# Spreading the read-back pairs among the computed ones, reordering the first chunk's loads, and loading the weights from another queue, in a fused attention and MLP kernel

## The chip, the cores and the metric

The kernel runs on one core of a Trainium2 chip. The metric is the device time of one execution in microseconds (us). Three runs of the kernel before took 1996.16, 1998.15 and 1998.2 us: the median is 1998.15 us.

## The reference

```python
# attention: u, v are (4, 3008, 256), z is (4, 3008, 64), float32
scores = (1.0 / S) * np.matmul(z, z.transpose(0, 2, 1))
attn = np.maximum(scores, 0.0) ** 2
x = (u * np.matmul(attn, v)).reshape(B * S, D)
# MLP on 12032 tokens: w_in is (256, 2048), w_out is (2048, 256)
h = x @ w_in
g = h * np.clip(h + 3.0, 0.0, 6.0) / 6.0
return (g @ w_out).astype(np.float32)
```

The scores are symmetric: the block of rows j and columns t is the transpose of the block of rows t and columns j. The two weights arrive as float64; the kernel reads them as pairs of 32-bit words.

## The kernel before, in words

**Tiles.** A batch has 3008 tokens, cut into 6 chunks of 512 columns (the last has 448); 4 batches make 24 chunks. For one chunk the 3008 rows are walked in 12 pairs of two 128-row tiles. The work of one pair in one chunk is a step: 24 x 12 = 288 steps, numbered g. Of every float32 operand a high part (fp32r) and the rest, a low part, are kept, and each product is made of three matmuls (low x high, high x low, high x high).

**A direct pair.** `scores` makes the block: 4 matmuls into a PSUM tile `s`, then ScalarE (ACT) applies the ReLU (`rt`) and the square in high form (`ah`), a square in full (`r2`, on ACT in the first three chunks, on VectorE, DVE, later), and DVE takes the rest (`al`). If the pair's rows belong to a later chunk (`keeps`), `keep` sends the full square to DRAM (`d<-r`, two transfers of 256 KB from SyncE's queue, SP), because its transpose is wanted there.

**A mirrored pair.** Where the pair's rows belong to an earlier chunk (`p // 2 < c`), nothing is computed: `fetch_pair` reads the kept block back (`l<-d`, four transfers of 128 KB on SP, two pairs ahead at most), `turn` transposes it on DVE (`rm`), ACT makes `ah` and DVE makes `al`. In chunk c the first 2c of 12 pairs are mirrored.

**The product with v.** `attend` adds the pair to the output `o`: 12 matmuls (two halves d, two tiles r, three products). The pairs of a chunk are taken in the order 0 to 11, so the mirrored ones all come first. After the last, DVE multiplies by u (`times_u`).

**The MLP.** From step `FIRST = 28` on, units of the MLP are put between the steps, some 1.4 a step: `up` (12 matmuls into `h`, then ReLU6 and the split) and `down` (12 matmuls into `y`).

**The order.** It is written out by hand in the loop at the end: in step g, `scores` for step g + `lead` (2 before step 28, then 1), `turn`, a number of weight operations, loads and splits for the next batch, `attend` of step g, units of the MLP. Engines run their instructions in that order.

**Weights.** They come in 16 pieces of 512 KB, two pieces ahead, each into one of the 5 buffers `r` that `rt`, `r2` and `rm` also use. A piece takes 8 DVE operations of `split64` and `finish64` (L101 to L133) and one copy on ACT (L117). `weight_work(n)` runs the next n of these: 1 before the first step, 2 a step in chunk 0, 4 a step up to step 27, then 5.

**The first chunk's loads.** z comes in 6 blocks, v in 12 pairs. In batch 0 v is loaded twice: as it is by SP, and rounded to the high part by GpSimd's queue (POOL), so that ACT needn't copy it; so are the z blocks 2 to 5. The loads of v, z, u and the weights stand in SP's queue between the `d<-r` and `l<-d`.

Of the kernel before, what the change touches and what calls it, by code (L numbers as in the profile page):

```python
# [13 lines left out]
B, S, D, DQK, DFF = 4, 3008, 256, 64, 2048  # L14
NT = B * S
P = 128
CH = 512
NCH = 6
# [12 lines left out]
def relu2_attention_then_hswish_mlp(  # L31
# [40 lines left out]
    def mm(out, lhsT, rhs, start, stop):  # L72
        nc.tensor.matmul(out, lhsT=lhsT, rhs=rhs, start=start, stop=stop)  # L73

    def split(hi, lo, raw, rounded=False):
        if not rounded:
            nc.scalar.copy(out=hi, in_=raw)  # L77
        nc.vector.tensor_tensor(out=lo, in0=raw, in1=f(hi), op=ALU.subtract)  # L78
# [69 lines left out]
    def fetch_w(kind, q):  # L148
        _, _, src, cols = w_piece(kind, q)
        if wide:  # L150
            raw = rpool.tile([P, 2, D, 2], U32, tag="r", name="wraw")
            nc.sync.dma_start(
                out=raw.rearrange("p k n w -> p k (n w)"),
                in_=src[:, :, 2 * cols.start:2 * cols.stop],
            )
        else:
            raw = rpool.tile([P, 2, D], F32, tag="r", name="wraw")
            nc.sync.dma_start(out=raw, in_=src[:, :, cols])
        raws["w", kind, q] = raw

    raws = {}
# [3 lines left out]
    def fetch_v(b, p):  # L165

        if b == 0 and p < NPAIR - 1:
            raw = vpool.tile([P, 2, D], F32, tag="vl", name="vraw")
        else:
            raw = stg.tile([P, 2, D], F32, tag="stg", name="vraw")  # L170
        vh = vpool.tile([P, 2, D], F32R, tag="vh", name="vh")
        vt[b, p] = vh
        raws["v", p] = raw
        j0 = p * 2 * P
        for dst, queue in ((raw, nc.sync), (vh, nc.gpsimd))[:1 if b else 2]:
            if p < NPAIR - 1:
                queue.dma_start(
                    out=dst, in_=v[b, j0:j0 + 2 * P, :].rearrange("(r q) d -> q r d", q=P)
                )
            else:  # L180
                queue.dma_start(out=dst[:, 0, :], in_=v[b, j0:j0 + P, :])
                for h in range(2):
                    queue.dma_start(out=dst[64 * h:64 * h + 64, 1, :], in_=v[b, j0 + P:S, :])

    def split_v(b, p):
        vh, raw = vt[b, p], raws.pop(("v", p))
        vl = vpool.tile([P, 2, D], F32R, tag="vl", name="vl")
        split(vh, vl, raw, rounded=b == 0)
        vt[b, p] = (vh, vl)

    def fetch_z(b, k):
        if b == 0:
            raw = xpool.tile([P, CH], F32, tag=("xh0", "xh1", "xl0", "xl1")[k % 4], name="zraw")
        else:
            raw = stg.tile([P, CH], F32, tag="stg", name="zraw")
        zx = zpool.tile([P, CH], F32R, tag="zx", name="zx")
        zy = zpool.tile([P, CH], F32R, tag="zy", name="zy")
        zt[b, k] = (zx, zy)
        raws["z", k] = raw
        cols = slice(k * CH, (k + 1) * CH)  # L200
        nc.sync.dma_start(out=raw, in_=zz[b, :, cols])
        if b == 0 and k > 1:
            nc.gpsimd.dma_start(out=zx[0:64], in_=zz[b, 0:64, cols])
            nc.gpsimd.dma_start(out=zy[64:128], in_=zz[b, 64:128, cols])
# [11 lines left out]
    def flush():  # L216
        urgent.clear()
        while late:
            late.pop(0)()

    kept, mirrored, turned, whole = {}, {}, {}, set()
    to_fetch = []

    def fetch_mirrored():

        while to_fetch and len(mirrored) < 2:
            b, c, p = to_fetch[0]
            if (b, p // 2, c) not in whole:
                return
            fetch_pair(*to_fetch.pop(0))  # L230
# [33 lines left out]
    def turn(b, c, p):  # L264

        if p // 2 >= c:
            return
        n = width(c)
        t = mirrored.pop((b, c, p))
        rn = rpool.tile([P, 2, CH], F32, tag="r", name="rm")[:, :, :n]  # L270
        nc.vector.transpose(  # L271
            out=rn.rearrange("p r (k e) -> p r k e", e=32),
            in_=t[:, :n // 32].rearrange("p k (r e) -> p r k e", r=2),
        )
        turned[b, c, p] = rn
        fetch_mirrored()

    def from_mirror(b, c, p):
        n = width(c)
# [79 lines left out]
    def av(b, c, p, d):  # L359

        n = width(c)
        if p == 0:
            bank = "y" if (b, c) == (0, 1) else "o"
            ot[d] = ps1.tile([P, CH], F32, tag=f"{bank}{d}", name=f"o{d}")
        o = ot[d][:, :n]
        ah, al = at[b, c, p]
        vh, vl = vt[b, p]
        dd = slice(d * P, d * P + P)
        for r in range(2):
            last = p == NPAIR - 1 and r == 1  # L370
            mm(o, vl[:, r, dd], ah[:, r, :n], p == 0 and r == 0, False)
            if not last:
                mm(o, vh[:, r, dd], al[:, r, :n], False, False)
            mm(o, vh[:, r, dd], ah[:, r, :n], False, last)
# [78 lines left out]
            nc.sync.dma_start(out=yt[e * P:(e + 1) * P, t0:t0 + n], in_=y[:, e, :n])  # L453

    chunks = [(b, c) for b in range(B) for c in range(NCH)]
    pairs = [(b, c, p) for b, c in chunks for p in range(NPAIR)]
    units = [("up", 0)]
    for q in range(NFP):
        units += [("up", q + 1)] if q + 1 < NFP else []
# [59 lines left out]
    def weight_work(n):  # L519
        for _ in range(n):  # L520
            next(w_ops, None)
# [39 lines left out]
    with tc.manual_schedule():  # L561
        nc.vector.memset(three, 3.0)
        fetch_z(0, 0)
        fetch_v(0, 0)
        split_z(0, 0)
        fetch_z(0, 1)
        fetch_v(0, 1)
        weight_work(1)
        split_v(0, 0)
        split_z(0, 1)  # L570
        scores(0, 0, 0)
        fetch_z(0, 2)
        fetch_v(0, 2)
        scores(0, 0, 1)
        fetch_v(0, 3)
        g_done = 2
        to_fetch += [(b, c, p) for b, c, p in pairs if p // 2 < c]
        g_turned = [2]
        for i, (b, c) in enumerate(chunks):
            ahead = b + 1 if c == NCH - 1 and b + 1 < B else None  # L580
            for p in range(NPAIR):
                g = i * NPAIR + p
                lead = 2 if g < FIRST else 1
                if i == 0:
                    if p + 1 < NPAIR:
                        split_v(0, p + 1)
                    if p % 2 == 0 and p // 2 + 2 < NCH:
                        split_z(0, p // 2 + 2)
                while g_done < min(g + lead + 1, len(pairs)):
                    scores(*pairs[g_done], square_on_act=i < 3)  # L590
                    g_done += 1
                if p > 3:
                    fetch_mirrored()
                if p < NPAIR - 1:
                    turn_next()
                if i == 0:
                    if p + 4 < NPAIR:
                        fetch_v(0, p + 4)
                    if p % 2 == 0 and p // 2 + 3 < NCH:
                        fetch_z(0, p // 2 + 3)  # L600
                    if p == 6:
                        load_u(*chunks[0])
                        load_u(*chunks[1])
                maybe_split()
                if g >= FIRST:
                    weight_work(5)
                elif p < NPAIR - 2:
                    weight_work(4 if i else 2)
                if ahead and p < NPAIR - 1:
                    if p:  # L610
                        split_v(ahead, p - 1)
                    if p < NPAIR - 2:
                        fetch_v(ahead, p)
                    if p % 2 == 1:
                        fetch_z(ahead, p // 2)
                    elif p:
                        split_z(ahead, p // 2 - 1)
                elif b and c == 0 and p < 4:
                    if p in (1, 2):
                        split_v(b, NPAIR - 3 + p)  # L620
                    if p < 2:
                        fetch_v(b, NPAIR - 2 + p)
                    if p == 2:
                        fetch_z(b, NCH - 1)
                    if p == 3:
                        split_z(b, NCH - 1)
                attend(b, c, p)
                turn_next()
                if p == NPAIR - 1:
                    avs[0] += 1  # L630
                total = len(pairs) - FIRST
                target = max(0, g + 1 - FIRST) * ((len(chunks) - 1) * NU - 4) // total
                mlp_units(target - units_done[0])
        mlp_units(1)
        maybe_split()
        mlp_units(len(chunks) * NU - units_done[0])
# [35 lines left out]
```

## Time and profile before

| | |
|---|---|
| median of 3 runs | 1998.15 us |
| the profiled execution: its own time | 1999.87 us |
| the profiled execution: span from first to last instruction | 1998.1 us |
| PE (TensorE) busy | 1960.8 us, 98% of the span |
| DVE, ACT busy | 1280.7 us (64%), 987.3 us (49%) |
| POOL busy | 14.2 us (26 instructions) |
| DMA | 178.14 MB, 89 GB/s over the span |
| mean granted TensorE clock | 0.992 |

PE is busy nearly throughout, so a change can only win where PE waits or runs below its full clock. Time is lost where the busy share of a stretch is below 1 or where PEclk is below 1.00.

### The profile page before, as it was taken

The numbers are of one execution on the slowest core, as the hardware profiler recorded it, in microseconds if no ns is written. First come the engines' busy times: TensorE is split into PE (matmuls) and PEld (weight loads), VectorE is DVE, ScalarE is ACT, GpSimd is POOL, SyncE is SP. The second block draws the span as 40 slices with busy tenths as digits, with TensorE's granted clock in tenths as the row PEclk, the third lists the DMA queues.
The fourth block names the chain that finished last, engine by engine and source line by source line (L and its number), as shares of the span: only waits on it lengthen the run. The fifth ranks groups of instructions, "written<-read, shape, count | busy, mean of one in ns | idle before, by whom it ended". The sixth has DMA issues, their size and how long they took to land.

```text
span 1998.1 us, 22059 instructions
## 1 busy us (share of the span) xinstructions
PE 1960.8 (98%) x8688; PEld 1637.4 (82%) x8688; DVE 1280.7 (64%) x1277; ACT 987.3 (49%) x1057; POOL 14.2 (1%) x26
## 2 busy tenths in 40 slices
PE   7899999999999999999999999999999999999999
PEld 5677788788888888888888888888888888888888
DVE  6798766676556566577565565657756565665654
ACT  6665444465444444456454454444555544444444
POOL 2000000000000000000000000000000000000000
PEclk8899999999999999999999999999999999999999
DMA  9754232424323233253332232324342223332300
GB/s 260 201 159 110 64 82 71 113 74 116 82 64 81 72 74 93 51 127 91 95 82 82 62 90 56 98 65 106 93 116 61 83 61 92 74 82 60 94 10 20
DMA packets 403271, 178.14 MB, mean 89 GB/s; under 512 B 250080, under 2 KB 385248, under 8 KB 403168
## 3 DMA queue, kind: packets, MB, share of 16 engines
q1 hardware_dynamic: 399232, 172.55, 34.3%
q0 software_dynamic: 3936, 4.20, 1.0%
q8 instruction: 68, 1.11, 0.2%
q14 instruction: 35, 0.29, 0.1%
HBM read 104.07 MB, written 72.61 MB: 88 GB/s over the span
## 4 chain that ended last, share of the span: by engine, by line
PE 89%; DVE 4%; DMA 3%; ACT 2%; issue 1%; SPq 1%; DVEq 0%; ACTq 0%
PE o L73 34%; PE h L73 24%; PE y L73 24%; PE s L73 7%; DMA zraw<-in_zz_dram 1%; DVE rm L271 1%; DMA vraw<-in_v_dram 1%; DVE al L287 1%; DVE rt L421 1%; ACT rt L420 0%; SPq L240 0%; ACT gh L77 0%; ACT rt L320 0%; DVE gl L78 0%; DMA d<-r 0%
## 5 line engine op out<-in xcount | busy, mean ns | idle before, releaser
L421 DVE SCALAR_TENSOR_TENSOR rt<-rt,h 128x1024 f32<-128x1024 f32 (+1 forms) x192 | 229.9, 1197 | 419.9 <-ACT rt L420 419.6
L420 ACT ACTIVATE rt<-h,three 128x1024 f32<-128x1024 f32 (+1 forms) x192 | 210.9, 1099 | 548.4 <-PE h L73 545.6
L73 PE MATMUL o<-ah,vl 128*128 128x512 f32 (+1 forms) x1152 | 448.5, 389 | 9.7 <-DVE vl L78 3.7
L73 PE MATMUL o<-ah,vh 128*128 128x512 f32 (+1 forms) x1152 | 447.6, 389 | 0.0
L73 PE MATMUL o<-al,vh 128*128 128x512 f32 (+1 forms) x1104 | 430.3, 390 | 7.8 <-DVE al L287 6.4
L73 PE MATMUL y<-gh,w_out_l 128*128 128x512 f32 (+1 forms) x768 | 296.2, 386 | 1.8 <-DVE w_out_l L133 1.7
L73 PE MATMUL y<-gl,w_out_h 128*128 128x512 f32 (+1 forms) x768 | 296.3, 386 | 1.0 <-DVE gl L78 1.0
L73 PE MATMUL h<-xh,w_in_l 128*128 128x512 f32 (+1 forms) x768 | 295.9, 385 | 0.0
L73 PE MATMUL y<-gh,w_out_h 128*128 128x512 f32 (+1 forms) x768 | 295.9, 385 | 0.0
L73 PE MATMUL h<-xl,w_in_h 128*128 128x512 f32 (+1 forms) x768 | 295.8, 385 | 0.0
L73 PE MATMUL h<-xh,w_in_h 128*128 128x512 f32 (+1 forms) x768 | 295.8, 385 | 0.0
L78 DVE TENSOR_TENSOR gl<-rt,gh 128x1024 fp32r<-128x1024 f32 (+1 forms) x192 | 230.6, 1201 | 80.5 <-ACT gh L77 77.9
L73 PEld LDWEIGHTS o<-ah,vl 128*128 128x128 f32 x1152 | 218.4, 190 | 57.6 <-ACT ah L285 5.8
L77 ACT CAST gh<-rt 128x1024 fp32r<-128x1024 f32 (+1 forms) x192 | 197.2, 1027 | 123.5 <-DVE rt L421 123.3
L73 PEld LDWEIGHTS o<-ah,vh 128*128 128x128 f32 x1152 | 218.6, 190 | 40.9
L73 PEld LDWEIGHTS o<-al,vh 128*128 128x128 f32 x1104 | 209.2, 190 | 51.5 <-DVE al L287 9.8
L320 ACT ACTIVATE rt<-s 128x1024 f32<-128x1024 f32 x168 | 171.2, 1019 | 131.9 <-PE s L73 126.9
L332 DVE TENSOR_TENSOR r<-rt 128x1024 f32<-128x1024 f32 (+1 forms) x140 | 169.9, 1214 | 95.8 <-ACT rt L320 95.8
L340 DVE TENSOR_TENSOR al<-r,ah 128x1024 fp32r<-128x1024 f32 x140 | 170.9, 1221 | 22.2 <-ACT r L330 8.7
L73 PEld LDWEIGHTS y<-gh,w_out_l 128*128 128x128 f32 x768 | 144.2, 188 | 29.9 <-DVE w_out_l L133 1.3
L73 PEld LDWEIGHTS y<-gl,w_out_h 128*128 128x128 f32 x768 | 144.2, 188 | 28.6 <-DVE gl L78 2.0
L287 DVE TENSOR_TENSOR al<-rm,ah 128x1024 fp32r<-128x1024 f32 (+1 forms) x120 | 141.1, 1176 | 40.0 <-ACT ah L285 39.9
(51 smaller groups left out, 1808.7 us busy)
## 6 DMA issues: line engine op xcount, KB each, us to landing
d<-r SPq DMA_DIRECT2D x220, 256.0 KB, 2.9
l<-d SPq DMA_DIRECT2D x320, 128.0 KB, 3.2
l<-d SPq DMA_DIRECT2D x160, 112.0 KB, 2.8
vraw<-in_v_dram SPq DMA_DIRECT2D x44, 256.0 KB, 3.4
u<-in_ut_dram SPq DMA_DIRECT2D x20, 512.0 KB, 4.3
out_dram<-y SPq DMA_DIRECT2D x40, 256.0 KB, 3.2
zraw<-in_zz_dram SPq DMA_DIRECT2D x24, 256.0 KB, 3.7
wraw<-in_w_in_dram SPq DMA_DIRECT2D x8, 512.0 KB, 4.5
```

The costliest lines, as they stand in the source:

```text
L73: nc.tensor.matmul(out, lhsT=lhsT, rhs=rhs, start=start, stop=stop)
L77: nc.scalar.copy(out=hi, in_=raw)
L78: nc.vector.tensor_tensor(out=lo, in0=raw, in1=f(hi), op=ALU.subtract)
L271: nc.vector.transpose(out=rn.rearrange("p r (k e) -> p r k e", e=32), in_=t[:, :n // 32].rearrange("p k (r e) -> p r k e", r=2),)
L287: nc.vector.tensor_tensor(out=al[:, :, :n], in0=rn, in1=f(ah[:, :, :n]), op=ALU.subtract)
L320: nc.scalar.activation(out=rn, in_=s[:, :, :n], func=AF.Relu, scale=1.0 / S)
L332: nc.vector.tensor_tensor(out=r2_of, in0=r_of, in1=r_of, op=ALU.mult)
L340: nc.vector.tensor_tensor(out=l_of, in0=r2_of, in1=h_of, op=ALU.subtract)
L420: nc.scalar.activation(out=rn, in_=h, func=AF.Relu, bias=three)
L421: nc.vector.scalar_tensor_tensor(out=rn, in0=rn, scalar=6.0, in1=h, op0=ALU.min, op1=ALU.mult)
```

## The change

1. `pairs_of(c)` gives the order of a chunk's pairs. In chunks 0 to 4 it begins with a direct pair and spreads the mirrored ones evenly among the direct ones; the last two places are direct. Chunk 1 goes 2, 3, 4, 5, 0, 6, 7, 8, 9, 1, 10, 11; chunk 2 goes 4, 5, 0, 6, 1, 7, 8, 2, 9, 3, 10, 11; chunk 5 and chunk 0 stay as they were. `av`, the list of pairs and `attend` follow that order.
2. In batch 0 v is loaded once, by SP; ACT makes the high part. The loads of z blocks 2 and 3 and of v pairs 2 and 3 come ahead of the first `scores`; those of z blocks 4 and 5 and of later v come at the start of a step, ahead of its `scores`. The loads of u come one step later.
3. The weights are loaded from POOL's queue. The first come in step 1. `weight_work` runs 2 operations in steps 1 to 9 of chunk 0; then, up to step 27, 5 in a step whose newest pair is direct and 1 where it is mirrored, none in a chunk's first step; from step 28 on 5, as before.

```diff
@@ fetch_w
-            nc.sync.dma_start(
+            nc.gpsimd.dma_start(
                 out=raw.rearrange("p k n w -> p k (n w)"),
                 in_=src[:, :, 2 * cols.start:2 * cols.stop],
             )
...
@@ fetch_v
-        for dst, queue in ((raw, nc.sync), (vh, nc.gpsimd))[:1 if b else 2]:
-            if p < NPAIR - 1:
-                queue.dma_start(
-                    out=dst, in_=v[b, j0:j0 + 2 * P, :].rearrange("(r q) d -> q r d", q=P)
-                )
...
+        if p < NPAIR - 1:
+            nc.sync.dma_start(
+                out=raw, in_=v[b, j0:j0 + 2 * P, :].rearrange("(r q) d -> q r d", q=P)
+            )
...
@@ split_v
-        split(vh, vl, raw, rounded=b == 0)
+        split(vh, vl, raw)
@@
+    def pairs_of(c):
+        if c == NCH - 1:
+            return list(range(NPAIR))
+        back, direct = list(range(2 * c)), list(range(2 * c, NPAIR))
+        order, gaps = direct[:1], len(direct) - 2
+        for k, p in enumerate(direct[1:]):
+            if k < gaps:
+                order += back[len(back) * k // gaps:len(back) * (k + 1) // gaps]
+            order.append(p)
+        return order
@@
-    pairs = [(b, c, p) for b, c in chunks for p in range(NPAIR)]
+    pairs = [(b, c, p) for b, c in chunks for p in pairs_of(c)]
@@ ahead of the loop
         fetch_z(0, 1)
         fetch_v(0, 1)
-        weight_work(1)
+        fetch_z(0, 2)
+        fetch_z(0, 3)
+        fetch_v(0, 2)
+        fetch_v(0, 3)
         split_v(0, 0)
         split_z(0, 1)
         scores(0, 0, 0)
-        fetch_z(0, 2)
-        fetch_v(0, 2)
         scores(0, 0, 1)
-        fetch_v(0, 3)
@@ in a step
                 if i == 0:
+                    if p + 4 < NPAIR:
+                        fetch_v(0, p + 4)
+                    if p < 2:
+                        fetch_z(0, p + 4)
...
-                if i == 0:
-                    if p + 4 < NPAIR:
-                        fetch_v(0, p + 4)
-                    if p % 2 == 0 and p // 2 + 3 < NCH:
-                        fetch_z(0, p // 2 + 3)
-                    if p == 6:
-                        load_u(*chunks[0])
-                        load_u(*chunks[1])
+                if i == 0 and p == 7:
+                    load_u(*chunks[0])
+                    load_u(*chunks[1])
                 maybe_split()
                 if g >= FIRST:
                     weight_work(5)
-                elif p < NPAIR - 2:
-                    weight_work(4 if i else 2)
+                elif 0 < p < NPAIR - 2:
+                    weight_work(2 if i == 0 else 1 if is_mirrored(*pairs[g_done - 1]) else 5)
...
-                attend(b, c, p)
+                attend(*pair)
```

**Where the instructions move.** The first place is SP's queue at the very start, batch 0, chunk 0 (`zraw`, `vraw` and `wraw` are loads of z, v and weights, `d01` the kept blocks of pairs 2 and 3). Before:

```order
L152 DMA wraw_118<-in_w_in_dram 128x2x512
L152 DMA wraw_120<-in_w_in_dram 128x2x512
L201 DMA zraw_141<-in_zz_dram 128x512
L177 DMA vraw_147<-in_v_dram 128x2x256
L177 DMA vraw_164<-in_v_dram 128x2x256
L257 DMA d01_184<-r2_181 512x1x128 x2
L177 DMA vraw_188<-in_v_dram 128x2x256
L201 DMA zraw_192<-in_zz_dram 128x512
```

With the change:

```order
L200 DMA zraw_116<-in_zz_dram 128x512
L200 DMA zraw_122<-in_zz_dram 128x512
L176 DMA vraw_128<-in_v_dram 128x2x256
L176 DMA vraw_131<-in_v_dram 128x2x256
L176 DMA vraw_167<-in_v_dram 128x2x256
L200 DMA zraw_170<-in_zz_dram 128x512
L270 DMA d01_193<-r2_190 512x1x128 x2
L176 DMA vraw_211<-in_v_dram 128x2x256
```

The weights are gone from this queue, and the fourth and fifth z block (`zraw_122`, `zraw_170`) stand ahead of the first kept block, where the fourth (`zraw_192`) stood behind it.

The second place is ACT in the same chunk, from pair 2 on. Before:

```order
L320 ACTIVATE rt_177<-s_172 128x1024
L329 ACTIVATE ah_178<-rt_177 128x1024
L330 ACTIVATE r2_181<-rt_177 128x8x4x32
L320 ACTIVATE rt_222<-s_217 128x1024
L329 ACTIVATE ah_223<-rt_222 128x1024
```

With the change:

```order
L336 ACTIVATE rt_186<-s_181 128x1024
L345 ACTIVATE ah_187<-rt_186 128x1024
L346 ACTIVATE r2_190<-rt_186 128x8x4x32
L77 CAST vh_129<-vraw_128 128x512
L336 ACTIVATE rt_228<-s_223 128x1024
```

Each step of chunk 0 has a fourth ACT instruction, the high part of v.

The third place is DVE where chunk 2 begins (`rm` and the `al` made of it are a mirrored pair's, the `al` of `r2` or `rt` a direct one's, `u` is `times_u`; `t0` and `wraw` are weight operations). Before:

```order
L271 STREAM_TRANSPOSE rm_972<-l_587 128x1024
L287 TENSOR_TENSOR al_992<-rm_972,ah_991 128x1024
L390 TENSOR_TENSOR u_449<-u_449,o0_649 128x512
L390 TENSOR_TENSOR u_449<-u_449,o1_656 128x512
L271 STREAM_TRANSPOSE rm_1007<-l_946 128x1024
L287 TENSOR_TENSOR al_1015<-rm_1007,ah_1014 128x1024
L271 STREAM_TRANSPOSE rm_1018<-l_974 128x1024
L131 TENSOR_TENSOR t0_846<-t0_846,w_out_h_93 128x512
```

With the change:

```order
L356 TENSOR_TENSOR al_958<-rt_956,ah_957 128x1024
L356 TENSOR_TENSOR al_982<-rt_980,ah_981 128x1024
L407 TENSOR_TENSOR u_480<-u_480,o0_642 128x512
L407 TENSOR_TENSOR u_480<-u_480,o1_649 128x512
L284 STREAM_TRANSPOSE rm_999<-l_673 128x1024
L303 TENSOR_TENSOR al_1007<-rm_999,ah_1006 128x1024
L356 TENSOR_TENSOR al_1031<-r2_1033,ah_1030 128x1024
L284 STREAM_TRANSPOSE rm_1040<-l_838 128x1024
```

The four mirrored pairs that opened the chunk one behind the other now have direct ones ahead of them and between them.

## Rows read from the trace of the kernel before

**Rows 1.** The page: the engines' busy time over the whole span, and the granted clock in 40 slices of 50 us each, in tenths.

```profile
PE 1960.8 (98%) x8688; PEld 1637.4 (82%) x8688; DVE 1280.7 (64%) x1277; ACT 987.3 (49%) x1057; POOL 14.2 (1%) x26
...
PEclk8899999999999999999999999999999999999999
```

**Rows 2.** Busy time of each engine by stretches of the span (us from its start): the stretch, its length, busy us and instructions of PE, PEld, DVE, ACT and POOL, then granted clock, DMA share and GB/s. The first stretch goes from the first matmul to the end of chunk 0's last product.

```profile
5.58:75.50 69.92, 55.98 (x191) 42.76 (x192) 45.11 (x60) 39.01 (x41) 9.67 (x16) 0.82 1.04 256
75.50:113.50 38.00, 38.00 (x166) 31.35 (x165) 34.16 (x50) 33.42 (x37) 0.00 (x0) 0.98 0.67 189
113.50:139.00 25.50, 22.50 (x87) 16.82 (x87) 22.34 (x30) 11.90 (x13) 0.00 (x0) 0.93 0.66 167
139.00:187.50 48.50, 48.50 (x216) 40.16 (x215) 40.47 (x55) 31.27 (x34) 0.00 (x0) 1.00 0.33 95
187.50:224.00 36.50, 31.95 (x135) 24.65 (x134) 32.87 (x41) 13.97 (x17) 0.00 (x0) 1.00 0.45 101
...
347.00:450.00 103.00, 99.11 (x449) 83.49 (x448) 73.87 (x80) 53.27 (x64) 0.00 (x0) 1.00 0.37 96
450.00:1950.00 1500.00, 1497.12 (x6698) 1256.39 (x6697) 936.23 (x877) 725.67 (x773) 0.00 (x0) 1.00 0.32 80
1950.00:1998.10 48.10, 44.67 (x217) 40.11 (x215) 20.03 (x20) 18.77 (x22) 0.00 (x0) 1.00 0.06 21
```

**Rows 3.** What PE waited for in the whole span: who waits, for whom, us in total, times, longest.

```profile
PE s L73 <- DVE zx L78: 7.4, 2, 5.6
PE o L73 <- DVE al L287: 6.4, 8, 1.8
PE s L73 <- issue: 6.2, 2, 3.9
PE o L73 <- DVE vl L78: 3.7, 2, 2.2
```

**Rows 4.** The chain of waits in the first 100 us: start, us, what.

```profile
1.65 6.68 DMA zraw<-in_zz_dram
...
18.76 11.65 DMA zraw<-in_zz_dram
...
50.99 3.90 issue
...
80.85 2.72 PE o L73 x12
83.57 0.91 PE s L73 x4
```

**Rows 5.** What ACT and DVE waited for in the first 76 us; two rows of ACT, then one of DVE.

```profile
ACT r L330 <- DMA d<-r: 6.2, 2, 3.9
...
ACT rt L320 <- DMA d<-r: 3.6, 1, 3.6
...
DVE zy L78 <- DMA zraw<-in_zz_dram: 11.5, 3, 6.4
```

**Rows 6.** DMA in the first 76 us: all packets, and issues with their number, KB each and median us from issue to landing.

```profile
DMA packets 26864, 18.91 MB, mean 249 GB/s; under 512 B 7917, under 2 KB 24045, under 8 KB 26861
...
d<-r SPq DMA_DIRECT2D x19, 256.0 KB, 5.1
...
vh<-in_v_dram POOLq DMA_DIRECT2D x11, 256.0 KB, 9.1
...
wraw<-in_w_in_dram SPq DMA_DIRECT2D x3, 512.0 KB, 11.0
```

**Rows 7.** The same from 80 to 112 us, in chunk 1.

```profile
d<-r SPq DMA_DIRECT2D x14, 256.0 KB, 2.9
wraw<-in_w_out_dram SPq DMA_DIRECT2D x3, 512.0 KB, 4.1
```

**Rows 8.** Groups of instructions from 76 to 112 us: line, engine, operation, out<-in, shapes, number, busy us, mean ns of one, idle time before.

```profile
L329 ACT ACTIVATE ah<-rt 128x1024 fp32r<-128x1024 f32 x10 | 10.6, 1063 | 0.3
L320 ACT ACTIVATE rt<-s 128x1024 f32<-128x1024 f32 x10 | 10.3, 1025 | 4.2 <-PE s L73 3.2 <-DMA d<-r 0.9
...
L340 DVE TENSOR_TENSOR al<-r,ah 128x1024 fp32r<-128x1024 f32 x7 | 8.5, 1219 | 0.0
...
L330 ACT ACTIVATE r<-rt 128x1024 f32<-128x1024 f32 x7 | 7.3, 1043 | 0.0
...
L106 DVE SCALAR_TENSOR_TENSOR t<-wraw,t 128x512 uint32<-128x512 uint32 x4 | 2.8, 693 | 0.1
...
L101 DVE TENSOR_SCALAR t<-wraw 128x512 uint32<-128x512 uint32 x5 | 2.1, 419 | 0.0
```

**Rows 9.** Instructions on the tile `vh` in the whole span: number, ns shortest/median/longest, first and last start. The first row is ACT's copy in batches 1 to 3, the second POOL's issue of the loads in batch 0.

```profile
L77 ACT CAST vh<-vraw x36: 598/618/622, 375.8 to 1465.2; 128x512 fp32r<-128x512 f32 x36
L177 POOL DMA_DIRECT2D vh<-in_v_dram x11: 726/730/844, 1.2 to 23.3; - x11
```

**Rows 10.** Instructions in order of time where chunk 2 begins: start, us, engine, line, operation, and in brackets the engine's idle time before and what ended it.

```profile
119.88 1.24 DVE L271 STREAM_TRANSPOSE rm<-l 128x1024 f32<-128x1024 f32 x1
121.21 1.05 ACT L285 CAST ah<-rm 128x1024 fp32r<-128x1024 f32 x1 [2.92 <-DVE rm L271]
122.29 1.23 DVE L287 TENSOR_TENSOR al<-rm,ah 128x1024 fp32r<-128x1024 f32 x1 [1.17 <-ACT ah L285]
123.43 1.28 DVE L390 TENSOR_TENSOR u<-u,o 128x512 f32<-128x512 f32 x2
```

More of the change, by code (lines that the diff above doesn't have):

```diff
@@ L157, in fetch_w @@
             raw = rpool.tile([P, 2, D], F32, tag="r", name="wraw")
-            nc.sync.dma_start(out=raw, in_=src[:, :, cols])
+            nc.gpsimd.dma_start(out=raw, in_=src[:, :, cols])
         raws["w", kind, q] = raw
@@ L174, in fetch_v @@
         j0 = p * 2 * P
-        for dst, queue in ((raw, nc.sync), (vh, nc.gpsimd))[:1 if b else 2]:
-            if p < NPAIR - 1:
-                queue.dma_start(
-                    out=dst, in_=v[b, j0:j0 + 2 * P, :].rearrange("(r q) d -> q r d", q=P)
-                )
[L180 to L183, printed above, removed]
+        if p < NPAIR - 1:
+            nc.sync.dma_start(
+                out=raw, in_=v[b, j0:j0 + 2 * P, :].rearrange("(r q) d -> q r d", q=P)
+            )
+        else:
+            nc.sync.dma_start(out=raw[:, 0, :], in_=v[b, j0:j0 + P, :])
+            for h in range(2):
+                nc.sync.dma_start(out=raw[64 * h:64 * h + 64, 1, :], in_=v[b, j0 + P:S, :])
     def split_v(b, p):
@@ L276, in turn, with is_mirrored @@
         fetch_mirrored()
+    def is_mirrored(b, c, p):
+        return p // 2 < c
     def from_mirror(b, c, p):
@@ L361, in av @@
         n = width(c)
-        if p == 0:
+        first = p == pairs_of(c)[0]
+        if first:
             bank = "y" if (b, c) == (0, 1) else "o"
@@ L370, in av @@
             last = p == NPAIR - 1 and r == 1
-            mm(o, vl[:, r, dd], ah[:, r, :n], p == 0 and r == 0, False)
+            mm(o, vl[:, r, dd], ah[:, r, :n], first and r == 0, False)
             if not last:
@@ L582, in relu2_attention_then_hswish_mlp @@
                 g = i * NPAIR + p
+                pair = pairs[g]
                 lead = 2 if g < FIRST else 1
                 if i == 0:
+                    if p + 4 < NPAIR:
+                        fetch_v(0, p + 4)
+                    if p < 2:
+                        fetch_z(0, p + 4)
                     if p + 1 < NPAIR:
```

## The prediction

> **What bounds the kernel now.** I read the page first: PE is busy for 98% of the span, and its clock is below full only in the first slices [rows 1]. Then the span by stretches, to see where the other 2% lie [rows 2]. At full clock a product takes 2.72 us and the four matmuls of a direct pair's scores 0.91 us, so a direct step needs 3.63 us of PE, a mirrored one 2.72 us, and one matmul 0.227 us [rows 4]. Chunk 0 holds 12 of each less two matmuls, 43.1 us, and takes 69.9 us: 26.8 us are lost, 13.9 in which PE is idle and 12.9 because the granted clock has a mean of 0.82, that is, stretches at 1.2 GHz among those at 2.4 [rows 2]. From 113.5 to 139 us 87 matmuls (19.7 us) take 25.5: 5.8 us lost. From 187.5 to 224 us 135 (30.6 us) take 36.5: 5.9 us lost. Between these nothing, and from 450 to 1950 us 2.9 us in all [rows 2]. So there are 38.5 us to win in the first 224 us, and next to nothing behind; the 3.9 us of the first chunk 5 and the 3.4 us of the tail lie where the order of pairs stays.
>
> What loses them: PE's waits name z's blocks (7.4 us), kept waiting by two loads that stand 6.7 and 11.7 us in the chain, and a piece of 3.9 us that the chain calls issue [rows 3, 4]. Behind these DVE waits 11.5 us for z, and ACT 9.8 us for a buffer `r` whose block is still on its way to DRAM [rows 5]. A block lands 5.1 us after issue there, against 2.9 us in chunk 1, because 18.91 MB move in 76 us, at 249 GB/s [rows 6, 7].
>
> **The change, part by part.**
>
> *Loads of chunk 0.* The second loading of v goes: 12 times 256 KB, 3.1 of 18.9 MB. The z blocks 3 and 4 stand ahead of the first kept block in SP's queue, so their 11.5 us of waiting should go [rows 5]. What is late next is ACT. It gets 12 copies of v at 0.62 us [rows 9], 7.4 us, and a step costs it 1.03 + 1.06 + 1.04 + 0.62 = 3.75 us [rows 8, 9], 0.12 us over PE's 3.63. Ten such steps and two weight copies (as long as v's) make 2.4 us, and the cold start with the first wait for an `al` I put at 2 us more, an estimate from the same rows (ACT's `ah` and DVE's `al` must follow before PE can go on, 2.3 us): 4.5 us lost is the lower end. The upper end is the DMA: 15.8 MB at the same 249 GB/s are 63.5 us, which end near 65 us instead of 75.5, so 16.3 us stay lost. The waits for `r` can't all go: eight `l<-d` still stand in SP's queue ahead of the kept block of pair 7, as before. I take 9.5 us, nearer to the lower end, since the waits on z and half of those on `r` vanish, and with them most of the idle time that brings the clock down to 1.2 GHz. **Gain 17.3 us**, ends 10.5 and 22.3. The copies on ACT I cost at nothing beyond that: ACT has 39.0 us of work in this stretch [rows 2], 46.4 with them, under some 53 us. Were that cover gone, it would be the whole 7.4 us.
>
> *Spread pairs and weights up to step 27.* Four mirrored pairs in a row cost PE its 5.8 us: `rm` 1.24, `ah` 1.05 and `al` 1.23 us follow each other, DVE idle 1.17 us for `ah`, so such a pair takes 3.5 us or more of a step in which PE has 2.72 us of work [rows 10]. Chunk 2 now begins with two direct pairs, and of the next four only two are mirrored. Against that, a direct step of chunk 1 gets five weight operations where it had four. An operation is 0.59 us (of eight, three at 0.42 and five at 0.69 [rows 8]), so DVE has 1.22 + 2.95 = 4.17 us in a step of 3.63 [rows 4, 8]. Seven such steps and two mirrored at 3.05 us exceed PE by 4.4 us; the three steps with no operations give 2.4 us back each. I leave 3 us lost. **Gain 2.8 us**, ends minus 1 and 5.8.
>
> *From step 28 to the last weight.* Up to step 27 the weights now get 18 + 37 + 11 = 66 operations, where they had 21 + 40 + 16 = 77. The 11 that are put off, 6.5 us, fall on a DVE that is idle 8.0 us from 139 to 187.5 us but only 3.6 us of the next 36.5 [rows 2]. For it speaks that the six mirrored pairs which open chunk 3 no longer stand together there. I leave 4.5 of the 5.9 us lost. **Gain 1.4 us**, ends minus 6.5 and 5.9.
>
> *The weights' queue.* SP loses 16 issues, POOL gets them, at 0.73 us each as for v [rows 9]; POOL does nothing else, so 11.7 us of issue lie beside everything. SP no longer stops for a free `r` ahead of a kept block; that gain is inside the terms above. What waits behind POOL's wait is the next weight alone, but behind DVE's wait for a weight stand all `al`.
>
> *The other batches.* A step there has 2.72 to 3.63 us of attention and over 3 us of MLP, which covers a mirrored pair's 3.5 us; nothing to win [rows 2], and 1.5 us either way.
>
> **Sum:** 17.3 + 2.8 + 1.4 = 21.5 us. Against the profiled execution, 1999.87 us with its span of 1998.1, that is 1978.4; that execution stands 1.7 us above the median of the runs, so against the median 1998.15 it is 1976.6 us. The ends together give 1962.6 and 1996.6, but they won't all fall on one side.
>
> **Rivals.**
>
> *The DMA stays the bound of chunk 0.* For it: the mean of 249 GB/s over 76 us [rows 6], and that pairs still write 512 KB a step in a shorter time, so `d<-r` may go on landing after 5 us, ACT go on waiting, and each idle stretch cost the clock again. Against it: 2.9 us in chunk 1 with the same writes [rows 7]. Then only 10.5 us come, and the rest nothing: 1987.6 us.
>
> *DVE gives part of it back.* PE reaches step 28 some 20 us earlier, with 11 operations more to do. If all 6.5 us show, 17.3 + 2.8 - 6.5 = 13.6 us remain: 1984.6 us. For it: DVE is 90% busy where 5.9 us are lost now [rows 2].
>
> *Slower: weights that come late through POOL.* A piece is fetched two ahead, that is, eight operations before it is needed, at five a step 1.6 steps or 5.8 us. Loads by POOL of half that size took 9.1 us to land in the first 76 us [rows 6]. If the full pieces do so throughout, each holds DVE for 3.3 us, with all `al` behind it; 12 pieces are loaded from step 12 on: 39.6 us, less the 17.3 us of chunk 0, 22.3 us slower: 2020.4 us. It turns from 1.4 us late a piece, at a landing of 7.2 us. Against it: those loads ran beside SP's at up to three ahead while weights by SP took 11.0 us, and later 4.1 us for a full piece [rows 6, 7].
>
> The Trainium skill (SBUF — State Buffer, section SBUF: two separate sides) speaks against the change in just this way: a VectorE instruction in a two-port mode locks GpSimd out of SBUF, so that GpSimd can't write the descriptors of its DMAs, and it tells to issue from SP or ACT instead. By that rule the loads would be late and the time be that of this rival. The trace doesn't bear it out so far: POOL's issues last 726 to 844 ns [rows 9], though DVE was busy for 45.1 of 69.9 us there [rows 2].
>
> *The change moves nothing*, because waits only take other names: 1998 us.
>
> **How the numbers follow.** The forecast gets 0.59, the DMA-bound chunk 0.16, DVE's giving back 0.13, late weights 0.08, nothing 0.04. The predicted time is the forecast's, 1976.6 us. The range 1966 to 1991 holds nearly all of the forecast and most of the next two. A measurement tells 0.2%, 4 us, from no change: faster by over that is 0.59 + 0.16 + 0.13, less 0.01 for the worst of the DMA's case, 0.87; within it 0.04; slower 0.09.
>
> **What would show it.** Right: chunk 0's last product ends near 60 us; DVE's waits on z gone, ACT's on `d<-r` below 5 us; the clock at 2.4 GHz for most of chunk 0; ACT over 85% busy there; no stop at the start of chunk 2; POOL with 24 loads. Wrong: the clock still falling three times in the first 60 us; DVE waiting for `wraw`; new waits of PE on `w_out_l` or `gl` before 210 us; more than 3 us lost in any 1000 us behind 450 us.

## The result and the profile after

The change makes the kernel slower: 2012.96 us median of 6 runs (2011.91 to 2014.09) against 1998.1 us for the kernel before, a ratio of 1.0076 [1.0065, 1.0086]. Forecast were 1976.6 us and faster. The profiled execution took 2013.18 us with a span of 2011.4, 13.3 us more than that of before.

The page answers to [rows 1]: the first two slices are nearly at full clock now, and the fifth, from 201 to 251 us, is not.

```profile
PE 1961.0 (97%) x8688; PEld 1637.5 (81%) x8688; DVE 1280.2 (64%) x1276; ACT 993.5 (49%) x1070; POOL 16.1 (1%) x28
...
PEclk9999899999999999999999999999999999999999
```

The stretches answer to [rows 2] (stretch, length, busy us and instructions of PE, PEld, DVE, ACT, POOL; granted clock, DMA share, GB/s). They are cut where chunk 0 ends and behind steps 27, 36 and 39.

```profile
3.00:63.60 60.60, 52.15 (x199) 40.80 (x200) 42.37 (x57) 48.76 (x57) 5.50 (x9) 0.94 0.93 245
63.60:131.10 67.50, 58.68 (x239) 45.71 (x238) 50.46 (x69) 43.14 (x48) 3.61 (x5) 0.95 0.55 145
131.10:192.20 61.10, 59.63 (x260) 48.25 (x259) 53.76 (x72) 34.35 (x37) 5.07 (x7) 1.00 0.46 121
192.20:234.20 42.00, 24.36 (x90) 18.84 (x89) 28.42 (x37) 12.80 (x15) 0.00 (x0) 0.80 0.22 49
234.20:454.00 219.80, 217.03 (x964) 181.64 (x963) 142.36 (x139) 106.07 (x118) 0.00 (x0) 0.99 0.35 87
454.00:1952.00 1498.00, 1493.64 (x6682) 1253.20 (x6681) 936.96 (x878) 723.18 (x771) 0.00 (x0) 1.00 0.33 80
```

Chunk 0's last product ends at 63.6 us instead of 75.5. From 63.6 to 131.1 PE idles 8.8 us, and from 192.2 to 234.2 it idles 17.6 of 42 us, at a mean clock of 0.80. What PE waited for, over the whole span, answers to [rows 3]:

```profile
PE y L73 <- DVE w_out_l L133: 9.9, 1, 9.9
...
PE h L73 <- DVE w_in_l L133: 7.7, 1, 7.7
...
PE s L73 <- DVE zx L78: 6.2, 1, 6.2
```

The 6.2 us are the first load of z. The two rows ahead of it are waits for the last DVE operation on a weight piece (L133), once for `h`, once for `y`. Before, PE waited 1.7 us in all for `w_out_l` and never for `w_in_l`. The two are the 17.6 us.

The chain of the first 70 us, against [rows 4], no longer names z's later blocks. It goes over ACT and four kept blocks on their way to DRAM, the first and the last of them here:

```profile
16.91 6.63 DMA d<-r
...
54.65 6.81 DMA d<-r
```

To see where time came and went I read when the product of each step ends, in both traces, and take the differences. By the end of chunk 0, and up to step 39, the new order has made the scores of two more pairs, since direct ones now open the next chunk; these 1.8 us (two times 0.91) are taken off, so the numbers compare equal work. Negative is gained (us); the term of the prediction stands beside.

| stretch | predicted | the change |
|---|---|---|
| to the end of chunk 0 | -17.3 | -13.7 |
| steps 12 to 27 | -2.8 | +7.3 |
| steps 28 to 39 | -1.4 | +19.0 |
| steps 40 to 287 | 0 | +0.3 |

### The profile page after: what moved, and what is told of

Its sections match the earlier page's. It is cut to its first block, busy times and chain, and to the rows that moved or that the text cites. A ratio compares the mean times of both kernels' runs of the same rounds, so it can differ in the third digit from the quotient of the medians.

```text
span 2011.4 us, 22062 instructions
## 1 busy us (share of the span) xinstructions
PE 1961.0 (97%) x8688; PEld 1637.5 (81%) x8688; DVE 1280.2 (64%) x1276; ACT 993.5 (49%) x1070; POOL 16.1 (1%) x28
## 4 chain that ended last, share of the span: by engine, by line
PE 87%; DVE 5%; ACT 4%; DMA 3%; issue 1%; SPq 0%; DVEq 0%; ACTq 0%
PE o L73 32%; PE h L73 24%; PE y L73 24%; PE s L73 6%; DMA d<-r 1%; ACT rt L336 1%; DMA zraw<-in_zz_dram 1%; ACT r L346 1%; ACT ah L345 1%; ACT rt L437 1%; DVE rt L438 1%; DVE gl L78 1%; DVE al L356 0%; DMA vraw<-in_v_dram 0%; DVE rm L284 0%
## 5 line engine op out<-in xcount | busy, mean ns | idle before, releaser
L73 PE MATMUL o<-ah,vl 128*128 128x512 f32 (+1 forms) x1152 | 447.2, 388 | 11.4 <-DVE vl L78 5.0
L356 DVE TENSOR_TENSOR al<-r,ah 128x1024 fp32r<-128x1024 f32 (+1 forms) x139 | 169.8, 1221 | 39.7 <-ACT r L346 26.2
L73 PEld LDWEIGHTS h<-xh,w_in_l 128*128 128x128 f32 x768 | 144.7, 188 | 35.9 <-issue 8.1
```

Of the source, the lines that this page charges most:

```text
L356: nc.vector.tensor_tensor(out=l_of, in0=r2_of, in1=h_of, op=ALU.subtract)
```

## The experiments

The question was which of three things costs the 26 us that the two middle rows lose: the numbers of weight operations in each step (66 called for by step 28, instead of 77), the new order of pairs, or POOL's queue. Results, with the gains by stretch as above (on equal work; medians and ratios are of all runs; the kernel before ran again beside the experiments, with medians of 1995.9 to 1997.1 us). The stretches are read from one profiled execution of each kernel. The runs of one kernel lie 1.2 to 6.4 us apart, so a difference of 2 or 3 us between two rows is not shown by the rows alone.

| kernel | median us | ratio to before | chunk 0 | 12 to 27 | 28 to 39 |
|---|---|---|---|---|---|
| the change | 2012.96 | 1.0076 | -13.7 | +7.3 | +19.0 |
| e1_counts | 1987.65 | 0.9956 [0.9941, 0.9971] | -13.3 | +0.2 | -0.6 |
| e9_counts_sp | 1986.37 | 0.9951 [0.9937, 0.9966] | -11.7 | -1.7 | -0.7 |
| e4_order | 1995.11 | 0.9991 [0.9981, 1.0] | -11.4 | +4.2 | +0.1 |
| e5_loads | 1989.76 | 0.9969 [0.9959, 0.9978] | -8.5 | -1.7 | +0.1 |
| e3_copy | 2013.35 | 1.0084 [1.0069, 1.0099] | -12.1 | +6.5 | +19.2 |
| e6_own | 2005.92 | 1.0053 [1.0038, 1.0068] | -17.0 | +2.7 | +19.3 |
| e2_six | 2006.5 | 1.0053 [1.0038, 1.0068] | -11.8 | +7.0 | +14.1 |
| e10_head | 2006.56 | 1.0053 [1.0038, 1.0068] | -12.7 | +8.2 | +11.4 |
| e11_two | 1993.78 | 0.9984 [0.9974, 0.9994] | -9.3 | +2.3 | -0.3 |
| e14_one_less | 1998.74 | 1.0007 [0.9998, 1.0017] | -11.1 | +2.4 | +7.8 |
| e12_own_counts | 1983.05 | 0.9931 [0.9916, 0.9946] | -17.7 | -0.6 | -0.6 |
| e13_own_counts_sp | 1985.66 | 0.9945 [0.993, 0.996] | -12.0 | -2.5 | -0.6 |

### The counts, the queue and the order

**e1_counts**: the change with the old numbers of weight operations, 77 by step 28 again.

```diff
-                elif 0 < p < NPAIR - 2:
-                    weight_work(2 if i == 0 else 1 if is_mirrored(*pairs[g_done - 1]) else 5)
+                elif i == 0 and 0 < p < NPAIR - 2:
+                    weight_work(3 if p < 4 else 2)
+                elif i and p < NPAIR - 2:
+                    weight_work(4)
```

> The change with the numbers of weight operations of before: 2 a step in chunk 0 (3 in steps 1 to 3, so that the total is the same), 4 a step in chunks 1 and 2 up to step 27, 77 in all by then instead of 66. Theory A (the numbers of operations cost the time: the last pieces come late at steps 38 and 39, 19.4 us there, and five a step lay ACT's copy of a weight behind DVE in steps 14 to 24, some 9 us): 2013 - 19 - 9 = 1985 us (1982 to 1990), PE's waits for w_in_l and w_out_l under 1 us. Rival B (weights come late because POOL loads them): the waits for w_in_l and w_out_l stay, over 2008 us. Rival C (mixed mirrored and direct pairs cost it): steps 12 to 27 still lose over 8 us, 1993 us or more.

Measured: 1987.65 us, 25.3 less than the change. The losses of both middle rows are gone. The stretches of steps 12 to 27 and 37 to 39:

```profile
64.00:124.60 60.60, 56.10 (x240) 44.08 (x238) 52.39 (x74) 43.20 (x47) 4.93 (x7) 1.00 0.68 167
...
185.60:208.00 22.40, 20.69 (x88) 15.99 (x86) 20.17 (x24) 12.11 (x14) 0.00 (x0) 1.00 0.23 48
```

The last takes 22.4 us for the work that takes 42.0 in the change. So the counts alone turn a gain into a loss.

**e9_counts_sp**: e1_counts with the weights loaded by SP (one word: `nc.sync` for `nc.gpsimd` in `fetch_w`).

> e1_counts (the change with the old numbers of weight operations, 1987.65 us) with the weights loaded by SP again. If POOL's queue is worth something in this order: 3 us or more slower than e1_counts. If not: within 2 us. If loads by POOL cost time (rival B): 3 us or more faster.

Measured: 1986.37 us, intervals that overlap. So POOL's queue is not what costs the change its 25 us. In e1_counts, a line of POOL:

```profile
L152 POOL DMA_DIRECT2D wraw<-in_w_in_dram x8 | 5.8, 727 | 65.8 <-DVE gl L78 13.2 <-DVE zx L78 10.7 <-DVE al L356 10.2
```

and the weight loads of the whole span (number, KB, median us from issue to landing):

```profile
wraw<-in_w_in_dram POOLq DMA_DIRECT2D x8, 512.0 KB, 5.6
wraw<-in_w_out_dram POOLq DMA_DIRECT2D x8, 512.0 KB, 5.4
```

and in e9_counts_sp:

```profile
wraw<-in_w_in_dram SPq DMA_DIRECT2D x8, 512.0 KB, 4.7
wraw<-in_w_out_dram SPq DMA_DIRECT2D x8, 512.0 KB, 4.5
```

Through POOL a piece lands 0.9 us later in the median, at 5.6 and 5.4 us, under the 7.2 us from which the rival would have begun.

**e4_order** and **e5_loads**: e4_order is e1_counts with the pairs in the old order 0 to 11 (`if c >= 0` for `if c == NCH - 1` in `pairs_of`); e5_loads has the weights on SP as well, so that only the loads of chunk 0 and the later first weights are new.

> The change with the numbers of weight operations of before and with the pairs in their old order 0 to 11; loads of chunk 0 and weights from POOL's queue as in the change. Against e1_counts it shows what the order alone does. If spreading is worth what the prediction took it for (the four mirrored pairs that open chunk 2 and the six of chunk 3): 3 to 8 us slower than e1_counts, some 1990 us. Rival C (spreading costs time): 3 us or more faster than e1_counts. If the order makes no difference: within 2 us of it.

> The kernel before with the new loads alone: v once with its high part from ACT, the new places of the loads of z, v and u, weights from SP's queue from step 1 on, the old order of pairs and the old numbers of weight operations (2 a step in chunk 0, 3 in steps 1 to 3, then 4). Against e4_order (1995.1 us), which has POOL's queue besides. If the queue is worth nothing: within 2 us of e4_order. If SP's stops for a free buffer were worth something: 3 us or more slower, 1998 us or more. If loads by POOL cost time (rival B): 3 us or more faster.

Measured: 1995.11 and 1989.76 us. The new loads alone, with SP, bring 0.3%. The order is no culprit: it brings 7.5 us with POOL (e4_order to e1_counts), 3.4 with SP (e5_loads to e9_counts_sp). But it doesn't bring it where it was forecast: with SP, steps 12 to 27 gain the same 1.7 us in either order, and the difference shows by the end of chunk 0, where chunk 1 opens. With the old order POOL is 5.4 us worse than SP, with intervals that do not overlap: the outcome that was named above for loads by POOL that cost time. Steps 12 to 27 lose 4.2 us where they gain 1.7. There, from 95 to 125 us, ACT in e4_order has a wait that e5_loads has not:

```profile
ACT rt L336 <- DMA d<-r: 3.2, 1, 3.2
```

and a kept block lands later, 3.8 us after issue, in e5_loads 2.6:

```profile
d<-r SPq DMA_DIRECT2D x5, 256.0 KB, 3.8
```

That SP, while it waits for a free `r`, keeps the weights from running beside the kept blocks is a reading; no run tests it. What the traces do show is where the queue counts. Chunk 1 (steps 12 to 23) takes 45.8 and 45.0 us with POOL (e4_order, e1_counts) and 41.3 and 43.0 with SP (e5_loads, e9_counts_sp); with buffers of their own for the weights, as in the last two runs below, it takes 43.0 with either queue. In chunk 0 POOL is ahead, by 1.6 to 5.7 us in the table. So the queue isn't neutral: two effects nearly cancel in the new order and don't in the old, and the loss hangs on the shared `r`. By what path is not shown.

### Steps 12 to 27

**e3_copy**: the change with ACT's copy (L117) of the newer piece kept back, so that it isn't run when an older piece is finished (`while len(copies) > pending` for `while copies` in `finish64`). ACT had waited 8.9 us for L114 at that copy, with `rt` behind it.

> The change with ACT's copy of a weight kept back: finish64 of one piece no longer issues the copy of the next piece, which then follows the next pair's squares, as it does before the change. Theory A2 (with five operations a step the copy is laid ahead of the next pair's rt on ACT while it waits for DVE's fourth operation behind this pair's al, so ACT and DVE take turns): ACT's waits of L117 for DVE t, 8.9 us in three from 75 to 125 us, fall below 2 us, steps 14 to 24 win 6 to 9 us, 2004 to 2007 us. Rival D (DVE has too much to do there, 4.17 us a step against PE's 3.63): the waits take another name, 2011 us or more. Rival B or A1 alone: 2013 us.

Measured: 2013.35 us, the same as the change. Of the copy's waits one of 1.2 us is left, and others have their time, ACT's and PE's from 64 to 130 us:

```profile
ACT rt L337 <- DMA d<-r: 5.1, 2, 3.2
ACT rt L337 <- PE o L73: 4.6, 1, 4.6
...
PE o L73 <- DVE al L357: 4.3, 5, 1.9
```

That theory fell. What stands behind `rt` in the change is a buffer: in order of time, before chunk 2,

```profile
110.23 0.62 ACT L117 CAST w_out_h<-t 128x512 fp32r<-128x512 f32 x1 [3.32 <-DVE t L114]
...
110.70 0.69 DVE L123 SCALAR_TENSOR_TENSOR w_out_l<-wraw 128x512 fp32r<-128x512 uint32 x1
...
111.47 1.02 ACT L336 ACTIVATE rt<-s 128x1024 f32<-128x1024 f32 x1 [0.62 <-DVE w_out_l L123]
...
113.64 0.50 PE L73 MATMUL o<-ah,vl 128*128 128x512 f32 x1 [2.06 <-ACT ah L345]
...
115.99 0.79 PE L73 MATMUL o<-al,vh 128*128 128x512 f32 x1 [1.85 <-DVE al L356]
```

L123 is the last operation that reads a raw piece; with it the piece's `r` comes free, and `rt` starts 0.08 us later. PE waits twice, and the granted clock is 0.5 (1.2 GHz) from 114.3 to 121.2 us.

**e6_own**: the change with two buffers of their own for the raw pieces, three left for `r`.

```diff
-    rpool = ctx.enter_context(tc.tile_pool(name="rpool", bufs=5))
+    rpool = ctx.enter_context(tc.tile_pool(name="rpool", bufs=3))
+    wrpool = ctx.enter_context(tc.tile_pool(name="wrpool", bufs=2))
...
-            raw = rpool.tile([P, 2, D, 2], U32, tag="r", name="wraw")
+            raw = wrpool.tile([P, 2, D, 2], U32, tag="wr", name="wraw")
```

> The change with two buffers of their own for the raw weights, the other uses of r keeping three of the five. Theory E (ACT's rt waits until DVE's operation L123 lets go of a weight's buffer, behind this pair's al and up to four other operations, so the pair that opens chunk 2 is 4 us late and the clock falls): that wait is gone, the end of step 24 comes 5 to 8 us sooner than in the change, step 28 too; what three buffers cost in the MLP is not the question, some 2007 us if nothing. Theory D (DVE is simply full in chunk 1 with five operations a step): the end of step 28 within 2 us of the change's 134.5 us, 2011 us or more.

Measured: 2005.92 us. Step 24, the first of chunk 2, ends at 112.9 us instead of 121.0; steps 12 to 27 lose 2.7 us instead of 7.3, and chunk 0 gains 3.3 us more. Steps 28 to 39 lose as before, so that is another cause.

### Steps 28 to 39

**e2_six**: the change with 6 operations a step from step 28 instead of 5 (`weight_work(6)`).

> The change with 6 weight operations a step from step 28 on instead of 5, nothing else. Theory A1 (the last pieces are split a step too late, because 11 operations fewer are done by step 28): the waits of PE for w_in_l and w_out_l, 17.6 us with a fall of the clock, go; 1996 us (1992 to 2000), and steps 12 to 27 stay as slow as they are. Rival B (loads by POOL come late): DVE can't go faster than the loads, 2010 us or more, with DVE waiting for wraw. Rival D (DVE is simply full from step 28 on): as much is lost spread over steps 28 to 38, over 2005 us.

**e10_head**: the change with 3 operations a step in chunk 0 instead of 2 (`3 if i == 0`), 75 by step 28.

> The change with 3 weight operations a step in chunk 0 instead of 2, so that 75 are done by step 28 instead of 66; five and one from chunk 1 on as in the change. Theory A1 (the stop at steps 38 and 39 comes only from being 11 operations behind when DVE is full): PE's waits for w_in_l and w_out_l, 17.6 us and a fall of the clock, go, steps 12 to 27 still lose 6 us or more, 1993 to 1998 us. If the five a step from step 28 on are too few whatever was done before: over 2005 us. If chunk 0 has no room on DVE: it ends 3 us or more later.

Measured: 2006.5 and 2006.56 us. In both the wait for `w_in_l` is gone, and the one for `w_out_l` stays, e2_six first:

```profile
PE y L73 <- DVE w_out_l L133: 9.3, 1, 9.3
```

```profile
PE y L73 <- DVE w_out_l L133: 7.1, 1, 7.1
```

Both waits were expected to go if being eleven operations behind were all; both times are over the 2005 us named for a DVE that is simply full. But the loss isn't spread over the steps, as it would be then: it sits in one wait. Ten operations (of the eleven) and nine are put back, and 9.3 and 7.1 of its 9.9 us stay, which doesn't look like DVE's amount of work. Counting in the program gives another cause. The unit `down` in step 38 needs w_out's seventh piece, whose last operation is the 127th called for. Before and in e1_counts 77 + 10 x 5 = 127 are called for by the end of step 37. The change has 66 + 50, e2_six 66 + 60 = 126, e10_head 75 + 50 = 125: there the last one is called for in step 38, and DVE takes it behind a unit's `rt` and `gl`, an `al`, a transpose and the split of x. The next two runs move one and two operations, some 35 steps earlier.

**e14_one_less**: e1_counts with one operation fewer (`3 if p < 3`), 126 by step 37.

> The changed kernel with the old counts of weight operations, but one operation fewer, in step 3 of chunk 0 (2 where the old counts have 3), so that all later ones stand one place later. Theory C: the last operation on w_out's seventh piece slips from the end of step 37 into step 38, behind an al, a transpose and the splits; PE waits 4 to 8 us for w_out_l about 205 us from the start, with part of it again in the clock: 1993 to 1998 us, where the old counts took 1987.65. Theory L: one operation of 0.6 us is put off, under cover: 1987 to 1989 us.

**e11_two**: e10_head with two more, in steps 1 and 2 (`(4 if p < 3 else 3) if i == 0`), 127 by step 37.

> The changed kernel with 4 weight operations in steps 1 and 2 of chunk 0 and 3 in steps 3 to 9, two more than in the run with 3 a step: 77 of them are called for by step 28, as before the change, but five and one a step stay in steps 12 to 27. Theory C (a threshold: the last operation on w_out's seventh piece has to be called for by step 37, or it stands behind the next pair's al and the splits of x, PE stops for it and its clock falls): the wait of y for w_out_l goes, step 39 ends 0 to 2 us after the kernel before instead of 8.7, and the whole takes 1997 to 2001 us. Theory L (only the amount of work on DVE counts): two operations are 1.2 us, so 2005 us and the wait stays at 5 us or more.

Measured: one operation less costs 11.1 us (1998.74 against 1987.65, a little over the 1998 expected), two more gain 12.8 us (1993.78 against 2006.56, below the 1997 expected). The theory of the threshold holds in both, that of the amount of work in neither. The same count settles the other wait: `up` in step 37 needs w_in's eighth piece, whose last operation is the 119th. The number called for by the end of the step before, and PE's wait (us) for that piece:

| kernel | by step 36, 119 needed | wait for `w_in_l` | by step 37, 127 needed | wait for `w_out_l` |
|---|---|---|---|---|
| before, e11_two, the runs with the old counts | 122 | none | 127 | none over 0.9 |
| e14_one_less | 121 | none | 126 | 8.1 |
| e2_six | 120 | none | 126 | 9.3 |
| e10_head | 120 | none | 125 | 7.1 |
| the change, e3_copy, e6_own | 111 | 7.7 | 116, and 4 called for by that `up` | 9.9 |

So the change is too late for two pieces, and each kernel stops just where its count falls short. DVE in e1_counts where step 37 ends:

```profile
199.90 0.69 DVE L133 TENSOR_TENSOR w_out_l<-t,w_out_l 128x512 fp32r<-128x512 f32 x1
200.51 1.21 DVE L438 SCALAR_TENSOR_TENSOR rt<-rt,h 128x1024 f32<-128x1024 f32 x1
202.84 1.22 DVE L78 TENSOR_TENSOR gl<-rt,gh 128x1024 fp32r<-128x1024 f32 x1 [1.12 <-ACT gh L77]
```

and in e14_one_less, with the matmul that waited:

```profile
205.22 0.68 DVE L131 TENSOR_TENSOR t<-t,w_out_h 128x512 f32<-128x512 f32 x1
205.83 1.22 DVE L438 SCALAR_TENSOR_TENSOR rt<-rt,h 128x1024 f32<-128x1024 f32 x1
208.15 1.23 DVE L78 TENSOR_TENSOR gl<-rt,gh 128x1024 fp32r<-128x1024 f32 x1 [1.11 <-ACT gh L77]
209.29 1.22 DVE L303 TENSOR_TENSOR al<-rm,ah 128x1024 fp32r<-128x1024 f32 x1
210.43 1.24 DVE L284 STREAM_TRANSPOSE rm<-l 128x1024 f32<-128x1024 f32 x1
211.59 1.25 DVE L78 TENSOR_TENSOR xl<-u,xh 128x512 fp32r<-128x512 f32 x2
212.76 0.69 DVE L133 TENSOR_TENSOR w_out_l<-t,w_out_l 128x512 fp32r<-128x512 f32 x1
...
213.59 0.76 PE L73 MATMUL y<-gh,w_out_l 128*128 128x512 f32 x1 [8.10 <-DVE w_out_l L133]
```

The one L133, 0.69 us long, slid behind five other groups of instructions and began 6.9 us later, and PE stood for 8.1 us. In the table that is 8.4 us in steps 28 to 39; 4.3 us more lie before (2.0 come back behind step 39), half of them in chunk 0, where PE waits 3.7 us for a `vl` and the clock falls at 52.7 us. That part wasn't expected. Whether it comes of the one operation or differs from execution to execution is not shown.

In the change DVE and PE take turns: DVE stands 5.8 us for PE's `h`, which has just waited 7.7 us for DVE.

```profile
208.49 0.69 DVE L133 TENSOR_TENSOR w_in_l<-t,w_in_l 128x512 fp32r<-128x512 f32 x1
209.10 0.42 DVE L101 TENSOR_SCALAR t<-wraw 128x512 uint32<-128x512 uint32 x1
215.36 1.22 DVE L438 SCALAR_TENSOR_TENSOR rt<-rt,h 128x1024 f32<-128x1024 f32 x1 [5.84 <-ACT rt L437]
```

### The version that beats both

**e12_own_counts** and **e13_own_counts_sp**: e1_counts with e6_own's buffers; e13_own_counts_sp has the weights on SP too.

> The changed kernel with the old counts, and the weights' raw pieces in two buffers of their own (r has three). In the changed kernel alone this ended chunk 0 3.3 us sooner and took 7 us off. If the buffers cost the old counts too: chunk 0's last product ends near 60.5 us instead of 64 and the whole takes 1983 to 1985 us. If they only hurt where five operations fall in a step: 1987 to 1988 us, as without.

> As the run before, with the weights loaded from SP's queue as in the kernel before the change. With own buffers SP no longer stops at a weight load for a free r, and the blocks to be kept stand behind them in the queue without harm: the same time as with POOL within 2 us, 1982 to 1986 us. If a weight load in SP's queue still held up what stands behind it, or POOL's issues cost something beside a busy DVE, the two would differ by 3 us or more, slower here in the first case and faster in the second.

Measured: 1983.05 us, 0.9931 [0.9916, 0.9946], the fastest, and 1985.66 us; the intervals overlap, so POOL or SP stays undecided here. Stretches of e12_own_counts, cut as those of the change (chunk 0, steps 12 to 27, then 37 to 39):

```profile
3.00:59.60 56.60, 49.30 (x199) 38.00 (x200) 44.21 (x60) 48.79 (x58) 6.22 (x10) 1.00 1.00 270
59.60:119.30 59.70, 56.14 (x239) 44.02 (x237) 52.24 (x74) 43.22 (x48) 3.61 (x5) 1.00 0.59 160
...
180.30:202.80 22.50, 20.76 (x88) 16.02 (x87) 20.24 (x24) 12.15 (x14) 0.00 (x0) 1.00 0.23 51
```

The clock doesn't fall again once it has risen. The start is not in these figures: the first matmuls, up to 8.7 us, start 0.43 us apart, where later ones start 0.23 us apart. This profiled execution is the fastest of its four runs (1980.54 us), so its span is 19.3 us shorter than that of before, more than the 14.1 of the medians. With the weights on POOL all four runs with own buffers are faster than all four of e1_counts, by 4.6 us in the median; on SP own buffers bring 0.7 us (e9_counts_sp to e13_own_counts_sp), which is within the noise.

## Why the prediction was wrong

**Chunk 0: right in kind, 3.6 us too high** (17.3 predicted, 13.7 measured). Chunk 0 ended at 63.6 us; "near 60" was forecast. For "ACT over 85% busy" there are 80% (48.8 of 60.6 us), or 85% of the 57.4 us from the first matmul. Sized wrong, at least in part, is the half of the waits on `r` that was to vanish. Waits of ACT from 0 to 64 us, to be read against [rows 5], and the kept blocks there, against [rows 6]:

```profile
ACT rt L336 <- DMA d<-r: 3.6, 2, 3.4
...
ACT r L346 <- DMA d<-r: 3.1, 1, 3.1
```

```profile
d<-r SPq DMA_DIRECT2D x19, 256.0 KB, 4.5
```

6.7 of 9.8 us stay, where below 5 was the sign of a right forecast. After the start the clock still falls once, from 29.0 to 35.8 us; the 14 matmuls of that time would take 3.2 us at 0.227 us each, so 3.6 us go there. e12_own_counts, whose clock doesn't fall again, gains 17.7. ACT's copies of v were priced right: 616 ns each, as in [rows 9]. In part it may have been the weights that held `r`: with their own buffers the term is 17.0 (e6_own) and 17.7 us (e12_own_counts), though with SP 12.0 (e13_own_counts_sp).

**Steps 12 to 27: wrong sign** (2.8 gained predicted, 7.3 lost). The working had DVE over PE by 4.4 us in the steps with five operations, and then gave "2.4 us back each" for the three steps without. That giving back is the step that failed. Steps 22 and 23, two of the three, take 3.6 and 3.2 us in the change and in e1_counts alike; PE is busy there with its own 3.63 us (two matmuls less in step 23), so the time that it has lost behind a late DVE can't return there. The other omission is that a piece holds one of five `r` until L123, so a DVE that is behind also stops ACT. Step 24, where chunk 2 opens, takes 9.5 us in the change, 6.4 before and 3.8 in e1_counts, and own buffers take 4.6 of the 7.3 us away (e6_own). The gain itself was sized too high as well. With four operations a step, 1.22 + 4 x 0.59 = 3.58 us, under PE's 3.63, the whole stretch comes to +0.2 (e1_counts): the stop where chunk 2 opens [rows 10] was to bring up to 5.8 us and brings 2.5 at step 24, and chunk 1 takes 45.0 us instead of 42.1. How the rest splits stays open: e11_two keeps the five and one, and loses only 2.3 us.

**From step 28 to the last weight: wrong by a mechanism** (1.4 gained predicted, 19.0 lost, where the worst end was 6.5). "The 11 that are put off, 6.5 us, fall on a DVE that is idle" prices operations by their length. That step failed. What decides is whether the last operation on a piece is called for by the step before the unit that needs it: one piece one operation too late costs 8.4 us (e14_one_less), and the change, too late for two pieces, loses 19.0. The numbers 77 and 66 stood in the prediction; which unit needs which operation was not counted. The rival "DVE gives part of it back" had the place, and a third of the price. "New waits of PE on `w_out_l`" before 210 us was named as a sign of a wrong forecast; what came was a wait on `w_in_l` up to 209.3 us, and the one on `w_out_l` from 216.9 to 226.8.

**The weights' queue: right for this order.** POOL's issues last 727 ns beside a DVE that is busy for 52.4 of 60.6 us (e1_counts, steps 12 to 27), and moving them to SP changes the whole by nothing that can be told; with the old order of pairs it gains 5.4 us (e4_order to e5_loads). The rule of the Trainium skill (SBUF — State Buffer, section SBUF: two separate sides), by which a VectorE instruction in a two-port mode would keep GpSimd from writing its descriptors, does not show in these runs: a piece lands 5.6 us after issue through POOL and 4.7 through SP. Which of the instructions here are in such a mode, if any, no run tells. The slower case came true for another reason than that rival's.

**The other batches: right**, 0.3 us in 248 steps.

## What to carry to other kernels

In a program whose order is written by hand, count what is finished by when, not only how long it takes: for each consumer the number of the operation it needs, and the number called for by then. Here one operation of 0.69 us, one place too late, began 6.9 us later and cost 8.4 us. And a buffer that is shared between a background job and the main chain can make the background job's delay the main chain's: with the weights on POOL buffers of their own brought 4.6 and 7.0 us, on SP nothing that can be told.

## What the runs showed that was not expected

- After a stop of 7 to 10 us PE starts again at the lower clock: in e14_one_less the matmuls behind the 8.1 us wait start 0.43 us apart, from 213.6 to 216.3 us, then 0.23 us. The granted clock is 0.5, that is 1.2 GHz, from 209.7 to 216.6 us, so 3 us of it hit work.
- Taking buffers away cost nothing: with three `r` instead of five (e6_own, e12_own_counts) the batches behind run as fast, within 1.3 us over 248 steps.
- Chunk 0 may answer to single operations: with one weight operation fewer there its gain is 2.2 us smaller (e1_counts to e14_one_less), with two more 3.4 us smaller (e10_head to e11_two), with waits of 3 to 4 us behind which the clock falls. Each figure is from one execution, and runs of one kernel differ by as much, so this is not shown.
